# Attention, mixing FFN and top-2 attention on one core: plain float32 value products for six odd heads, an earlier start and an earlier last u

## The chip, the cores and the metric

The kernel runs on one core of a Trainium2 chip. The metric is the device time of one execution in microseconds (us), the median of the runs given. The engines are named as in the profile: PE is TensorE (matrix products; PEld its weight loads), DVE is VectorE, ACT is ScalarE, POOL is GpSimd, SP is SyncE, whose queue issues nearly all DMAs.

## The reference

Three blocks run one after another over 4 batches of 576 positions. The first is a causal attention with decay and 8 heads of 64, the second a mixing step and a feed-forward network over 512 channels, the third a top-2 gated attention of 4 experts.

```python
log_f = np.log(np.clip(f, 0.0001, 1.0)); cum = np.cumsum(log_f, axis=-1)
scores = scale * q @ k.T + cum[:, :, :, None] - cum[:, :, None, :]   # causal
attn = exp(scores - max); attn = attn / (attn.sum + 1e-09)
x = attn @ v                                                     # block 1
u = x + (x.T @ U @ V).T; x = u + np.maximum(u @ w_ch1, 0) @ w_ch2  # block 2
...                                                              # block 3: out += mask * w * ((a @ v) @ wo[e])
```

The change touches block 1 and the step from it into block 2.

## The kernel before, in words

Block 1 has 32 heads, taken in 16 pairs (`p`), an even and an odd head (`h = 2p + j`). All its work is written as events: `put(h, us, do)` (line 978) places a step at `us` in the nominal slot of 8.4 us of head `h`, `early(us, do)` (line 981) before slot 0, and the events are issued in the order of these times (line 1321). Every engine, and SP's queue, then works in that order; a time in the list decides only who stands behind whom. Slots as measured have other lengths. The pools are small: PE's results of scores and of row maxima share two buffers (`ps2`), the value product has one (`av`), the loaded q, k, v of a pair have two places.

For each head, in its slot: `score_products` (line 264) makes the transposed scores in two parts, u = 0 of 576 columns and u = 1 of two times 512; ACT takes the exponentials (line 305). Each of the three pieces is then split into float16 halves: ACT copies the high one (`high_part`, line 310), DVE subtracts it (`low_part`, line 313). In the next slot `weighted_values` (line 332) multiplies them with v, which is scaled by a power of two and split in the same way: 15 blocks, each as high by high, high by low and low by high, so 45 products of 64 or 65 columns; column 65 of v is ones and gives the sum of the row. `row_scales` and `normalise` (lines 386 and 406) divide.

v's power of two is `value_events` (line 1055): DVE's largest value (`value_max`, line 349), a transpose, three small steps on DVE (`value_power`), a product that spreads it (`value_spread`, line 369), a reciprocal, then ACT's high half and DVE's low half of both heads at once (lines 380 and 383). For pair 0 this chain, up to the spreading product, stands before slot 0.

The row maxima of head `h + 2` are made in slot `h` (`max_events`, line 1018): products `ua` and `ub` on PE (lines 202 and 220), five masked maxima on DVE (lines 207 and 228). In slot `h + 1` PE turns them (`mt`, line 234) and a DMA puts them as a row into the head's operand (`put_row`, line 237), which the scores of slot `h + 2` read. `split_events` (line 1085) prepares q and k of a pair: ACT's rounded copies, SP's moves of them between partitions (`split_moves`, line 855) and POOL's remainders.

In slots 0 to 9 PE also has `busy` products (line 1277) on a constant tile, whose results nobody reads: 8, 14 and 8 a slot. From pair 5 on, groups of block 2's first quarter (`fill`, 12 products each, lines 680 and 696) stand among the heads. After the last head comes a dense stretch of such groups. Block 2 reads u, the mixed output (`mix_events`, line 1138), which is stored to DRAM per pair and read back per batch: `ffn_begin` (line 624) reads three quarters of a batch's first half early and takes the fourth from the tile when its pair is mixed, for batches 1 and 2; batch 3 is read whole by `ffn_prepare` at the start of the dense stretch (line 1391), and `cast_some` (line 666) converts it in two pieces on ACT and DVE.

Of the kernel before, what the change touches and what calls it, by code (L numbers as in the profile page):

```python
# [18 lines left out]
P = 128  # L19
# [6 lines left out]
NT = 5  # L26
# [56 lines left out]
def kernel(  # L83
# [171 lines left out]
    def exponent_tiles(pl_, n, eng=nc.gpsimd):  # L255

        made = []
        for i in range(n):
            two = pl_.tile([P, 2 * 1600 + 64], F16, name=f"ph{i}")
            eng.memset(two[:, 3200:3264], 0.0)  # L260
            made.append((two, two[:, 1600:3264]))
        return made
# [69 lines left out]
    def weighted_values(ph, pl, vh, vl, its=(0, NT), av=None):  # L332
# [26 lines left out]
    def value_power(at_):  # L359
        counter[1] += 1  # L360
        full = ars[counter[1] % 2]
        ar = full[0:1, :]
        nc.vector.tensor_reduce(ar, at_[:], AX.X, OP.max)
        nc.vector.tensor_scalar(ar, ar, 1.0e-30, None, OP.max)
        nc.vector.tensor_scalar(ar.bitcast(I32), ar.bitcast(I32), 0x7F800000, None,
                                OP.bitwise_and)
        return full

    def value_spread(full):
        rp = psf.tile([P, 1], F32, name="rsp", tag="f")  # L370
        nc.tensor.matmul(rp[:], spread[:], full[:].bitcast(BF16)[:, 1:2], start=True, stop=True)
        return rp
# [13 lines left out]
    def row_scales(av, rs):  # L386

        den = small.tile([P, NT], F32, name="den")
        total = av()[:, :, 64:65].rearrange("p t o -> p (t o)")
        nc.vector.tensor_scalar(den[:], total, 1.0e-9 * PSCALE, rs()[:, 0:1], OP.add, OP.mult)  # L390
# [430 lines left out]
    khigh = att.tile([P, S], F32R, name="khigh")  # L821
    vhs = []
    for i in range(2):
        vh_ = hpool.tile([P, 2, NT, 65], F16, name=f"vh{i}")
        vl_ = hpool.tile([P, 2, NT, 64], F16, name=f"vl{i}")
        nc.vector.memset(vh_[:, :, :, 64:65], 1.0)
        vhs.append((vh_, vl_))
    NPAIR = B * NP
# [26 lines left out]
    def split_moves(p, j):  # L855

        if p >= NPAIR:
            return
        qa, qb, ka, kb = pair_heads(p)[j]
        src = f32(chl[2 * p + j:2 * p + j + 1]) if p < 2 else cdram[2 * p + j]  # L860
        nc.sync.dma_start(f32(ka[64:66, 0:S]), src)
        if p == j == 0:
            load_qk(1)
        if j == 0:
            nc.sync.dma_start(f32(qb[lo_, :]), f32(qa[lo_, :]))
            nc.sync.dma_start(f32(kb[hi_, :S]), f32(ka[lo_, :S]))
        else:
            nc.sync.dma_start(f32(qa[lo_, :]), f32(qb[hi_, :]))
            nc.sync.dma_start(f32(ka[lo_, :S]), f32(khigh[hi_, :]))
            nc.sync.dma_start(f32(kb[lo_, :S]), f32(khigh[hi_, :]))  # L870

# [112 lines left out]
    def head_events(h):  # L984

        p, j = divmod(h, 2)
        hb = pair_heads(p)[j]
        ph, pl = exps[h % 2]
        st = {}
# [16 lines left out]

        def attend():
            vh, vl = vhs[p % 2]
            st["av"] = weighted_values(ph, pl, vh[:, j], vl[:, j])

        put(h + 1, 4.55, attend)
        finish = row_scales(lambda: st["av"], lambda: st_rs[p])
        for us in (6.15, 6.35):
# [4 lines left out]
    def max_events(h):  # L1018
# [13 lines left out]
        if h < 2:  # L1032
            for us, n in ((8.5, 0), (8.7, 1)) if h == 0 else ((12.3, 0), (13.2, 1)):
                early(us, rows, n)
            early((9.2, 12.9)[h], lambda: last_max(st[0], st["mx"]))
            for n, t in enumerate((3, 2, 1, 0)):
                early((9.8, 13.7)[h] + 0.6 * n, first, t)
        else:
# [16 lines left out]
    def value_events(p):  # L1055
# [21 lines left out]
        put(h, 1.95, step, "am", None, value_max)  # L1077
        put(h, 4.54, step, "amt", "am", value_turn)
# [6 lines left out]
    def split_events(p):  # L1085
# [755 lines left out]
    def attend_slot(h, t, its=None, room=None, after=()):  # L1841
# [200 lines left out]
```

## Time and profile before

| what | us |
|---|---|
| median of 3 runs (lowest, highest) | 815.67 (814.83, 819.93) |
| the profiled execution, its own time | 815.98 |
| its span, first to last instruction | 814.2 |
| block 1 with its start, to the first score product / to the end of slot 12 | 17.02 / 129.57 |
| the whole first block, to the dense stretch, about | 298 |

The span is of one execution; times in the rows are from its start. A busy share counts any instruction in progress. PE's instructions overlap, so its busy time runs past the end of the streaming; the time from one start to the next is what a product costs in a stream. The releaser behind an idle time is inferred from semaphores and names what came last by the profile.

### The profile page before, as it was taken

Reading aid. Unit: us, or ns where it says so; the run is one execution under the profiler, and the core shown is the slowest. Engines: PE = TensorE matmul, PEld = TensorE weight load, DVE = VectorE, ACT = ScalarE, POOL = GpSimd, SP = SyncE. Lnnn points to the kernel's source line nnn. Section 1 sums busy time; section 2 is a strip of 40 time slices with the busy share of each in tenths; the row PEclk is TensorE's granted clock in tenths of the full one; section 3 lists DMA queues with packets and bytes.
Section 4 is the critical chain, followed back from the end, with each engine's and each line's share of the span. In section 5 each row is a group of like instructions: output and inputs, shape, how many; then the busy total and the mean of one; then the engine's idle time right before and its main releaser. Section 6 shows DMA issues by size and latency. Waiting matters only on the chain.

```text
span 814.2 us, 19790 instructions
## 1 busy us (share of the span) xinstructions
PE 763.0 (94%) x7726; PEld 658.8 (81%) x7726; DVE 605.5 (74%) x1671; ACT 433.2 (53%) x875; POOL 149.7 (18%) x248
## 2 busy tenths in 40 slices
PE   3888889999999989999899999999999889999997
PEld 3788879999999989977677777777778778888874
DVE  6988999998999948988873586366644557887873
ACT  6877887887787724637231242113311335676563
POOL 9643332423322000000002000000000511111110
PEclk9999999999999999999999999999999989999999
DMA  6565564666655044963230404400103547455422
GB/s 186 149 189 175 158 195 145 184 191 171 175 160 161 25 160 136 311 191 107 85 115 33 146 32 149 157 2 1 59 30 89 135 104 185 107 131 129 104 71 94
DMA packets 63694, 104.37 MB, mean 128 GB/s; under 512 B 5824, under 2 KB 39984, under 8 KB 63600
## 3 DMA queue, kind: packets, MB, share of 16 engines
q1 hardware_dynamic: 63232, 102.45, 42.7%
q8 instruction: 61, 1.00, 0.5%
q10 hardware_dynamic: 368, 0.66, 0.3%
q14 instruction: 33, 0.27, 0.1%
HBM read 53.25 MB, written 23.74 MB: 95 GB/s over the span
## 4 chain that ended last, share of the span: by engine, by line
PE 48%; DVE 5%; DMA 3%; ACT 1%; issue 1%; SPq 0%; ACTq 0%; DVEq 0%
PE cps L696 15%; PE hps L680 14%; PE pq L1550 5%; PE pv L1592 3%; PE sc L285 3%; PE po L1644 2%; DMA yl<-yhalves 1%; PE ub L220 1%; PE av L341 1%; PE av L345 1%; PE av L343 1%; DVE yc L702 1%; DVE w16a L537 1%; DMA ust<-udram 1%; PE ua L202 1%
## 5 line engine op out<-in xcount | busy, mean ns | idle before, releaser
L685 ACT ACTIVATE hh<-hps 128x288 f16<-128x288 f32 (+1 forms) x128 | 52.5, 410 | 221.0 <-PE hps L680 195.1
L686 DVE SCALAR_TENSOR_TENSOR hl<-hps,hh 128x288 f16<-128x288 f32 (+1 forms) x128 | 58.1, 454 | 81.6 <-ACT hh L685 81.2
L228 DVE CUSTOM_DVE_ANT_0 ub<-ub,maskm 128x448 f32<-128x448 f32 x192 | 82.2, 428 | 2.6 <-PE ub L220 1.1
L285 PE MATMUL sc<-qa,ka 128*128 128x288 f32 (+4 forms) x288 | 73.6, 316 | 4.2 <-DVE mx L207 2.2
L341 PE MATMUL av<-vh,ph 128*128 128x65 f16 x720 | 71.0, 195 | 0.3 <-DVE o L407 0.3
L343 PE MATMUL av<-vl,ph 128*128 128x64 f16 x720 | 70.6, 193 | 0.0
L345 PE MATMUL av<-vh,ph 128*128 128x65 f16 x720 | 70.5, 193 | 0.0
L702 DVE SCALAR_TENSOR_TENSOR yc<-cps,back,yc 128x288 f32<-128x288 f32 x96 | 49.4, 514 | 25.3 <-PE cps L696 22.4
L341 PEld LDWEIGHTS <-ph 128*128 128x128 f16 x720 | 65.8, 97 | 1.2 <-DVE o L407 0.6
L343 PEld LDWEIGHTS <-ph 128*128 128x128 f16 x720 | 66.1, 99 | 0.3
L345 PEld LDWEIGHTS <-ph 128*128 128x128 f16 x720 | 66.1, 98 | 0.0
L285 PE MATMUL sc<-qb,kb 128*128 128x288 f32 (+4 forms) x288 | 64.9, 307 | 0.0
L207 DVE CUSTOM_DVE_ANT_0 ua<-ua,maskm 128x576 f32<-128x576 f32 x48 | 36.5, 761 | 32.5 <-PE ua L202 27.8
L305 ACT ACTIVATE aside<-sc 128x512 f32<-128x512 f32 (+1 forms) x75 | 45.3, 617 | 26.6 <-PE sc L285 24.4
L285 PEld LDWEIGHTS sc<-qa,ka 128*128 128x128 f32 x288 | 50.0, 194 | 7.9 <-issue 3.3
L313 DVE TENSOR_TENSOR ph<-aside,ph 128x512 f16<-128x512 f32 (+1 forms) x75 | 55.1, 747 | 1.7 <-ACT ph L310 1.7
L285 PEld LDWEIGHTS sc<-qb,kb 128*128 128x128 f32 x288 | 53.6, 193 | 1.6
L313 DVE TENSOR_TENSOR ph<-pf,ph 128x512 f16<-128x512 f32 (+1 forms) x69 | 49.0, 722 | 6.4 <-ACT ph L310 6.4
L696 PE MATMUL cps<-hh,w16b 128*128 128x288 f16 x256 | 48.3, 286 | 0.8 <-DVE hl L686 0.8
L696 PE MATMUL cps<-hh,w16a 128*128 128x288 f16 x256 | 48.3, 286 | 0.0
L696 PE MATMUL cps<-hh,w1lf 128*128 128x288 f16 x256 | 48.3, 286 | 0.0
L680 PEld LDWEIGHTS <-w16a 128*128 128x128 f16 x384 | 37.4, 98 | 13.2 <-issue 3.8
(268 smaller groups left out, 2325.9 us busy)
## 6 DMA issues: line engine op xcount, KB each, us to landing
raw<-in_w_dram SPq DMA_DIRECT2D x32, 512.0 KB
ust<-udram SPq DMA_DIRECT2D x14, 576.0 KB
ydram<-yc SPq DMA_DIRECT2D x10, 576.0 KB
aside<-in_qk_dram SPq DMA_DIRECT2D x8, 576.0 KB
room<-in_qk_dram SPq DMA_DIRECT2D x8, 576.0 KB
udram<-ustage SPq DMA_DIRECT2D x16, 288.0 KB
ydram<-ust SPq DMA_DIRECT2D x8, 576.0 KB
yc<-ydram SPq DMA_DIRECT2D x8, 576.0 KB
```

Of the source, the lines that this page charges most:

```text
L228: nc.vector.tensor_tensor_reduce(ub[:, bk, off:off + w], ub[:, bk, off:off + w], maskm[:, S - w:S], 1.0, NEG, OP.add, OP.max, mx[:, t:t + 1])
L285: nc.tensor.matmul(ps[:, bk, off:off + w], wa, xa, start=bk not in banks[:n], stop=bk not in banks[n + 1:])
L305: nc.scalar.activation(pf[:, 0:S].rearrange("p (c n) -> p c n", c=2) if whole else pf[:, 0:n], view, AF.Exp, scale=ISC)
L313: nc.vector.tensor_tensor(pl[:, o0:o0 + n], pf[:, 0:n], ph[:, o0:o0 + n], OP.subtract)
L341: nc.tensor.matmul(av[:, it, :], ph[:, c:c + P], vh[:, jt, :], start=first, stop=False)
L343: nc.tensor.matmul(av[:, it, 0:64], ph[:, c:c + P], vl[:, jt, :], start=False, stop=False)
L345: nc.tensor.matmul(av[:, it, :], pl[:, c:c + P], vh[:, jt, :], start=False, stop=last)
L680: nc.tensor.matmul(ph[:], wa[:, k, fs], xa[:, k], start=n == 0, stop=n == 3 * KT - 1)
L685: after(lambda: nc.scalar.activation(hh[:], ph[:], AF.Relu), lambda: nc.vector.scalar_tensor_tensor(hl[:], ph[:], 0.0, high, OP.max, OP.su ...
L686: lambda: nc.vector.scalar_tensor_tensor(hl[:], ph[:], 0.0, high, OP.max, OP.subtract))
L696: nc.tensor.matmul(pc[:], wa[:, t, dsl], xa[:], start=n == 0, stop=n == 3 * FT - 1)
L702: nc.vector.scalar_tensor_tensor(yc[:, d, :], pc[:], back, yc[:, d, :], OP.mult, OP.add)
```

## The change

For the odd heads of pairs 0 to 5 (`NPLAIN = 6`) the exponentials are written in float32 into the tile that else holds the halves, with no split, and v's second head is loaded straight into a float32 tile with its column of ones; `plain_values` makes 15 plain float32 products, in two parts (rows 0 to 2 at 2.0 and 3 to 4 at 4.55 of the next slot). v's scale then covers the first head alone. Pair 0's scale moves from before slot 0 into slot 0, and its factor into the power step. Head 1's moves and pair 1's preparation are reordered. `busy` goes to 4 a slot, and 10 more in odd slots. `ffn_begin` also runs for batch 3.

```diff
-        nc.vector.tensor_scalar(ar, ar, 1.0e-30, None, OP.max)
+        nc.vector.tensor_scalar(ar, ar, 1.0e-30, 1.0 / VEXP, OP.max, OP.mult)
...
+    def plain_values(whole, vw, its, av=None):
+        if av is None:
+            av = ps1.tile([P, NT, 65], F32, name="av")
+        for it in range(*its):
+            order = list(range(it + 1)) if it < NT - 1 else [0, 4, 1, 2, 3]
+            for jt in order:
+                c = J_OFF[jt] + (it - jt) * P
+                nc.tensor.matmul(av[:, it, :], whole[:, c:c + P], vw[:, jt, :],
+                                 start=jt == order[0], stop=jt == order[-1])
+        return av
...
     def load_v(p):
-        if p < NPAIR:
+        if p < NPLAIN:
+            nc.sync.dma_start(places[p % 2][1][:, 0], v[p // NP, p % NP][:, 0])
+        elif p < NPAIR:
             nc.sync.dma_start(places[p % 2][1], v[p // NP, p % NP])
+    def load_second(p):
+        nc.sync.dma_start(vws[p % 2][:, 1, :, 0:64], v[p // NP, p % NP][:, 1])
...
-                st["pf", n] = exponentials(view, n_), o0, n_
+            if plain:
+                to = whole[:, o0:o0 + n_]
+                nc.scalar.activation(to if u else to.rearrange("p (c n) -> p c n", c=2), view,
+                                     AF.Exp, scale=ISC)
+            else:
+                st["pf", n] = exponentials(view, n_), o0, n_
...
             put(h, te, exp_, n)
+            if plain:
+                continue
...
-        put(h + 1, 4.55, attend)
+        if plain:
+            put(h + 1, 2.0, attend, (0, 3))
+            put(h + 1, 4.55, attend, (3, NT))
+        else:
+            put(h + 1, 4.55, attend)
...
-            early(12.6, lambda: put_row(hb, st["mt"]))
+            early(12.6, lambda: put_row(hb, st["mt"], True))
...
-            early(11.7, step, "amt", "am", value_turn)
-            early(13.9, step, "full", "amt", value_power)
-            early(14.9, step, "rp", "full", value_spread)
-            put(0, 0.2, factor)
-            put(0, 4.95, lambda: value_high(vr, st_rs[p], vh))
+            put(0, 4.54, step, "amt", "am", value_turn)
+            put(0, 5.6, step, "full", "amt", value_power)
+            put(0, 6.0, step, "rp", "full", value_spread)
+            put(0, 6.5, factor)
+            put(0, 6.6, lambda: value_high(vr, st_rs[p], vh))
...
+        if p < NPLAIN:
+            put(2 * p - 1, 4.6, load_second, p)
-    FIRST_SPLITS = ((5.8, 6.5, 7.5), (7.1, 8.8, 10.3), (11.6, 14.7, 14.8), (13.2, 19.3, 19.2))
+    FIRST_SPLITS = ((5.8, 6.5, 7.5), (7.1, 7.8, 10.3), (13.0, 14.7, 14.8), (14.2, 19.3, 19.2))
...
     for h in range(10):
-        put(h, 0.54, busy, 8)
-        put(h, 2.1, busy, 14)
-        put(h, 3.9, busy, 8)
+        put(h, 0.54, busy, 4)
+        if h % 2:
+            put(h, 2.1, busy, 10)
...
-    for b in (1, 2):
+    for b in (1, 2, 3):
         put(8 * b + 8, 4.0, ffn_begin, b)
```

On SP's queue before slot 0, the DMAs from the load of pair 0's q and k on stand in this order before (`chl` are the decay rows, `khigh` the rounded k of an odd head, `mr` the row of maxima):

```order
L836 DMA aside<-in_qk_dram 128x1152
L840 DMA aside<-in_v_dram 128x640
L861 DMA ka_130<-chl 2x1x576
L836 DMA room<-in_qk_dram 128x1152
L865 DMA qb_129<-qa_128 64x576
L866 DMA kb_131<-ka_130 64x576
L861 DMA ka_134<-chl 2x1x576
L868 DMA qa_132<-qb_133 64x576
L869 DMA ka_134<-khigh 64x576
L870 DMA kb_135<-khigh 64x576
L244 DMA qa_128<-mr 1x5x128
```

and so in the change:

```order
L856 DMA aside<-in_qk_dram 128x1152
L860 DMA aside<-in_v_dram 128x320
L892 DMA ka_128<-chl 2x1x576
L903 DMA qa_130<-qb_131 64x576
L904 DMA ka_132<-khigh 64x576
L892 DMA ka_132<-chl 2x1x576
L856 DMA room<-in_qk_dram 128x1152
L886 DMA qb_127<-qa_126 64x576
L887 DMA kb_129<-ka_128 64x576
L909 DMA kb_133<-khigh 64x576
L243 DMA qa_126<-mr 1x5x128
```

Head 1's two moves and its decay rows now stand before pair 1's load (`room`) and before head 0's two moves.

On DVE, in slot 6, from the division of head 4's output to the maxima of head 8, before (`ph_148` is the odd head's tile, `vl_161` v's low half, `am` its largest value):

```order
L407 TENSOR_TENSOR room<-av,rn 128x5x64
L938 TENSOR_TENSOR ul<-ustage,uh 128x288 x2
L313 TENSOR_TENSOR ph_148<-aside,ph_148 128x512 x2
L383 SCALAR_TENSOR_TENSOR vl_161<-aside,rs,vh_160 128x640
L351 TENSOR_REDUCE am<-room 128x1
L434 SCALAR_TENSOR_TENSOR wst<-raw,wst 128x512
L435 SCALAR_TENSOR_TENSOR wst<-raw,wst 128x512
L1242 TENSOR_TENSOR w1l<-wst,w1h 128x4x128
L313 TENSOR_TENSOR ph_146<-aside,ph_146 128x576
L207 ISA ua,mx_98<-ua,maskm 128x2x288
```

and in the change:

```order
L422 TENSOR_TENSOR room<-av,rn 128x5x64
L977 TENSOR_TENSOR ul<-ustage,uh 128x288 x2
L395 SCALAR_TENSOR_TENSOR vw_158<-aside,rs,vw_158 128x320
L363 TENSOR_REDUCE am<-room 128x1
L449 SCALAR_TENSOR_TENSOR wst<-raw,wst 128x512
L450 SCALAR_TENSOR_TENSOR wst<-raw,wst 128x512
L1304 TENSOR_TENSOR w1l<-wst,w1h 128x4x128
L313 TENSOR_TENSOR ph_144<-aside,ph_144 128x576
L206 ISA ua,mx_96<-ua,maskm 128x2x288
```

The odd head's two subtractions of 512 are gone (its third stood in the slot before), and v's low half is 320 wide.

On SP's queue at the end of the heads and the start of the dense stretch, before (`ustage` is a pair's mixed output):

```order
L943 DMA udram<-ustage 128x576 x2
L647 DMA ust<-udram 128x4x288
L546 DMA ust<-udram 128x4x288 x4
L761 DMA ydram<-ust 512x1x288
L647 DMA ust<-udram 128x4x288
L761 DMA ydram<-ust 512x1x288
```

and in the change:

```order
L982 DMA udram<-ustage 128x576
L644 DMA ust<-udram 128x3x288
L561 DMA ust<-udram 128x4x288 x4
L982 DMA udram<-ustage 128x576
L985 DMA ust<-udram 128x288
L776 DMA ydram<-ust 512x1x288
```

Three quarters of batch 3's u are read before the last pair's store, and the four loads for the other batches (line 546, 561) now stand before that store too.

## Rows read from the trace of the kernel before

**Rows 1.** The page: busy time of each engine in the span.

```profile
PE 763.0 (94%) x7726; PEld 658.8 (81%) x7726; DVE 605.5 (74%) x1671; ACT 433.2 (53%) x875; POOL 149.7 (18%) x248
```

**Rows 2.** Busy time by stretch, slots 0 to 12; columns: us, engines, PEclk, DMA share, GB/s.

```profile
17.02:23.91 6.89, 6.89 (x56) 6.55 (x55) 4.02 (x11) 3.57 (x7) 5.91 (x8) 1.00 0.71 203
23.91:33.28 9.37, 6.67 (x104) 6.06 (x101) 8.94 (x23) 8.47 (x18) 6.71 (x8) 1.00 0.61 175
33.28:50.30 17.02, 14.86 (x217) 13.87 (x218) 14.91 (x47) 12.53 (x26) 8.11 (x8) 1.00 0.51 140
50.30:65.77 15.47, 14.38 (x220) 13.72 (x219) 14.30 (x44) 13.26 (x28) 5.61 (x5) 1.00 0.68 197
65.77:84.78 19.01, 16.39 (x220) 15.33 (x218) 16.78 (x48) 15.13 (x31) 6.10 (x5) 0.91 0.55 160
84.78:102.24 17.46, 14.84 (x220) 13.82 (x218) 16.70 (x48) 15.17 (x32) 6.12 (x5) 1.00 0.61 175
102.24:121.95 19.71, 16.19 (x195) 15.12 (x194) 19.00 (x57) 17.40 (x37) 7.04 (x5) 1.00 0.65 195
121.95:129.57 7.62, 7.62 (x95) 7.49 (x95) 7.52 (x17) 6.26 (x13) 2.02 (x2) 1.00 0.48 135
```

**Rows 3.** Waits of PE, 23 to 123 us: us in total, times, longest.

```profile
PE mt L234 <- DVE mx L228: 7.6, 7, 1.5
```

**Rows 4.** PE's products: timeline (start, us, [idle]) and groups by form (busy, mean ns).

```profile
60.34 0.94 PE L1280 MATMUL some<-every 128*128 128x128 bf16 x14
61.13 1.28 PE L895 MATMUL gp<-room,ut 128*96 128x128 f32 x10
63.53 0.21 PE L341 MATMUL av<-vh,ph 128*128 128x65 f16 x1
64.91 0.41 PE L912 MATMUL up<-ident,room 128*128 128x128 f32 x2
...
L895 PE MATMUL gp<-room,ut 128*96 128x128 f32 x80 | 10.1, 273 | 0.0
L285 PEld LDWEIGHTS sc<-qb,kb 128*128 128x128 f32 x288 | 53.6, 193 | 1.6
```

**Rows 5.** DVE in slot 6 (timeline), and ACT's high copies in slots 1 to 11 (group).

```profile
68.28 0.68 DVE L313 TENSOR_TENSOR ph<-aside,ph 128x512 f16<-128x512 f32 x1
68.88 0.88 DVE L383 SCALAR_TENSOR_TENSOR vl<-room,rs,vh 128x640 f16<-128x640 f32 x1
69.68 0.81 DVE L351 TENSOR_REDUCE am<-aside 128x1 f32<-128x640 f32 x1
...
L310 ACT CAST ph<-aside 128x512 f16<-128x512 f32 x16 | 9.7, 619 | 0.0
```

**Rows 6.** The start: timelines of PE, SP's queue and ACT.

```profile
13.93 0.82 PE L202 MATMUL ua<-ka,qa 127*128 127x288 f32 x2 [1.23 <-POOL ka L167]
16.92 0.16 PE L371 MATMUL rsp<-ar,spread 128*128 128x1 bf16 x1 [1.26 <-DVE ar L365]
...
7.28 0.35 SPq L836 DMA_DIRECT2D room<-in_qk_dram  x1
10.23 0.55 SPq L869 DMA_DIRECT2D ka<-khigh  x1
...
21.93 0.60 ACT L305 ACTIVATE aside<-sc 128x512 f32<-128x512 f32 x1 [1.41 <-PE sc L285]
```

**Rows 7.** PE's first score product of slot 12.

```profile
121.95 0.37 PE L285 MATMUL sc<-qa,ka 128*128 128x288 f32 x1 [1.30 <-DMA qa<-mr]
```

**Rows 8.** The start of the dense stretch: SP's queue, ACT, PE, and a stretch as in rows 2.

```profile
297.39 0.60 SPq L647 DMA_DIRECT2D ust<-udram  x1
...
301.91 1.24 ACT L670 CAST uh<-ust 128x576 fp32r<-128x576 f32 x2 [3.43 <-DMA ust<-udram]
...
303.97 0.16 PE L482 MATMUL rsp<-ar,every 128*128 128x1 bf16 x1 [2.63 <-DVE ar L477]
...
305.06:308.47 3.41, 3.41 (x16) 3.41 (x16) 2.06 (x8) 0.00 (x0) 0.00 (x0) 0.50 0.79 280
```

More of the change, by code (lines that the diff above doesn't have):

```diff
@@ L44 @@
 FIRST = 15.6
+NPLAIN = 6
 PER_PAIR = (0,) * 5 + (3, 3, 3, 3, 4, 4, 4, 4, 3, 3, 2)
@@ L128 @@
     nc.gpsimd.memset(every[:], 1.0)
-    spread = const.tile([P, P], BF16, name="spread")
-    nc.gpsimd.memset(spread[:], 1.0 / VEXP)
     ars = []
@@ L258, in exponent_tiles @@
         for i in range(n):
-            two = pl_.tile([P, 2 * 1600 + 64], F16, name=f"ph{i}")
-            eng.memset(two[:, 3200:3264], 0.0)
-            made.append((two, two[:, 1600:3264]))
+            one_ = pl_.tile([P, 1664], F32, name=f"ph{i}")
+            eng.memset(one_[:, 1600:1664], 0.0)
+            two = one_[:].bitcast(F16)
+            made.append((two, two[:, 1600:3264], one_))
         return made
@@ L370, in value_spread @@
         rp = psf.tile([P, 1], F32, name="rsp", tag="f")
-        nc.tensor.matmul(rp[:], spread[:], full[:].bitcast(BF16)[:, 1:2], start=True, stop=True)
+        nc.tensor.matmul(rp[:], every[:], full[:].bitcast(BF16)[:, 1:2], start=True, stop=True)
         return rp
@@ L389, in row_scales @@
         total = av()[:, :, 64:65].rearrange("p t o -> p (t o)")
-        nc.vector.tensor_scalar(den[:], total, 1.0e-9 * PSCALE, rs()[:, 0:1], OP.add, OP.mult)
+        if rs() is None:
+            nc.vector.tensor_scalar(den[:], total, 1.0e-9 * PSCALE, None, OP.add)
+        else:
+            nc.vector.tensor_scalar(den[:], total, 1.0e-9 * PSCALE, rs()[:, 0:1], OP.add, OP.mult)
         yield
@@ L821 @@
     khigh = att.tile([P, S], F32R, name="khigh")
-    vhs = []
+    vhs, vws, firsts = [], [], []
     for i in range(2):
[L824 to L827, printed above, removed]
+        v_ = hpool.tile([P, 2 * NT * 65], F32, name=f"vw{i}")
+        vws.append(v_[:].rearrange("p (a t d) -> p a t d", a=2, t=NT))
+        nc.vector.memset(vws[i][:, 1, :, 64:65], 1.0)
+        n0, n1 = 2 * NT * 65, 2 * NT * (65 + 64)
+        vhs.append((v_[:].bitcast(F16)[:, 0:n0].rearrange("p (a t d) -> p a t d", a=2, t=NT),
+                    v_[:].bitcast(F16)[:, n0:n1].rearrange("p (a t d) -> p a t d", a=2, t=NT)))
+        firsts.append([v_[:].bitcast(F16)[:, n * NT:(n + k) * NT].rearrange(
+            "p (a t d) -> p a t d", a=1, t=NT) for n, k in ((0, 65), (65, 64))])
+        nc.vector.memset(firsts[i][0][:, :, :, 64:65], 1.0)
     NPAIR = B * NP
@@ L858, in split_moves, with rows @@
             return
+        if j == 2:
+            qa, qb, ka, kb = pair_heads(p)[0]
+            nc.sync.dma_start(f32(qb[lo_, :]), f32(qa[lo_, :]))
+            nc.sync.dma_start(f32(kb[hi_, :S]), f32(ka[lo_, :S]))
+            return
         qa, qb, ka, kb = pair_heads(p)[j]
         src = f32(chl[2 * p + j:2 * p + j + 1]) if p < 2 else cdram[2 * p + j]
-        nc.sync.dma_start(f32(ka[64:66, 0:S]), src)
-        if p == j == 0:
-            load_qk(1)
+        def rows():
+            nc.sync.dma_start(f32(ka[64:66, 0:S]), src)
         if j == 0:
+            rows()
+            if p == 0:
+                return
             nc.sync.dma_start(f32(qb[lo_, :]), f32(qa[lo_, :]))
             nc.sync.dma_start(f32(kb[hi_, :S]), f32(ka[lo_, :S]))
[L867 to L870, printed above, removed]
+            return
+        if p:
+            rows()
+        nc.sync.dma_start(f32(qa[lo_, :]), f32(qb[hi_, :]))
+        nc.sync.dma_start(f32(ka[lo_, :S]), f32(khigh[hi_, :]))
+        if p == 0:
+            rows()
+            load_qk(1)
+            split_moves(0, 2)
+        nc.sync.dma_start(f32(kb[lo_, :S]), f32(khigh[hi_, :]))
     def split_low(p, j, which=(0, 1)):
@@ L987, in head_events @@
         hb = pair_heads(p)[j]
-        ph, pl = exps[h % 2]
+        ph, pl, whole = exps[h % 2]
+        plain = j == 1 and p < NPLAIN
         st = {}
@@ L1032, in max_events @@
         if h < 2:
-            for us, n in ((8.5, 0), (8.7, 1)) if h == 0 else ((12.3, 0), (13.2, 1)):
+            for us, n in ((8.5, 0), (8.7, 1)) if h == 0 else ((11.3, 0), (12.3, 1)):
                 early(us, rows, n)
-            early((9.2, 12.9)[h], lambda: last_max(st[0], st["mx"]))
+            early((9.2, 12.45)[h], lambda: last_max(st[0], st["mx"]))
             for n, t in enumerate((3, 2, 1, 0)):
-                early((9.8, 13.7)[h] + 0.6 * n, first, t)
+                early((9.8, 13.1)[h] + 0.6 * n, first, t)
         else:
```

28 lines of the change are left out of this document (19 added, 9 removed).

## The prediction, made before the changed kernel was run

> **What bounds the kernel now.** I read each engine's share of the span first (PE 94%) [rows 1], then its busy time in stretches cut where TensorE (PE) begins a head's scores, which I call slots [rows 2], then what PE waited for in them [rows 3]. From slot 12 on PE is the bound: 7.62 us busy of 7.62. In slots 1 to 11 no engine is full alone: in slots 8 and 9 VectorE (DVE) is busy 16.70 of 17.46 us, ScalarE (ACT) 15.17, PE 14.84. PE's longest wait there is for the row maxima that DVE writes: 7.6 us in 7 waits, 1.5 at most [rows 3]. So these slots are set by DVE, with PE standing behind it, and part of PE's busy time is filling: 300 `busy` products in slots 0 to 9, at 0.056 us 16.8 in all [rows 4]. Two more places count. Before slot 0, PE waits for a move of head 1 and then for a chain on v's scale [rows 6]. At the end of the attention PE stands still for 2.63 us and then runs at the lower clock level [rows 8].
>
> **What the change costs and saves, part by part.** All sums are against the profiled execution, 815.98 us (span 814.2); the median of the runs shown is 815.67, 0.3 less, inside their spread of 5 us.
>
> *Engine loads of a pair of slots.* On PE the six odd heads give up 45 float16 products for 15 float32 ones. The 45 take 1.38 us, from the first start to that of the transposes behind them (63.53 to 64.91) [rows 4]. The nearest float32 row is the mixing product with U: its five products stand in the trace as ten passes, each with its own weight load. Ten passes take 1.28 us, and with the last one's own 0.27 taken off that is 0.112 a step, the first of them being longer than the rest; I read 0.11. Those passes stream 128 columns and load 96 of weights; the new ones stream 65 and load 128. If a pass went by its columns it would take 0.055; if load and stream did not overlap, the load's 0.193 [rows 4]. I take 0.11, the nearest row: 30 x 0.11 = 3.3, so 1.9 us more per odd head.
>
> The row shows float32 loads of 0.193 us against float16 products that start 0.031 us apart. [...]
>
> The `busy` products go from 30 a slot to 4 in even and 14 in odd slots: 42 fewer per pair, 0.056 each by 0.94 us for 14 of them with a tail of 0.16 [rows 4], 2.35 us less. Net on PE per pair: -0.45.
>
> On DVE each odd head loses its three subtractions: 512 wide they start 0.60 apart (68.28 to 68.88), the 576 wide one an eighth more, 1.87 together; v's low part (0.80 from start to start) and its largest value (0.81, of which such rows overlap 0.08) are made on half the columns [rows 5], 0.76 less. That is 2.6 us less per pair. ACT loses three copies of 0.62 or a little more [rows 5]: about 1.9.
>
> So per pair, in us, PE / DVE after the change: slots 2+3 14.4 / 12.3, slots 4+5 13.9 / 11.7, slots 6+7 14.2 / 14.2 (PE there also loses the 1.7 that the lower clock cost: granted 0.91 over 19 us), slots 8+9 14.4 / 14.1 [rows 2]. Now the largest load takes 96% of the pair in slots 8+9 and as little as 88% in slots 2+3 and 6+7. With 88% the four pairs take 64.6 us, with 100% 56.9, against 68.96 now: a gain of 4.3 to 12.1. I take 96%, since the waits of PE for the maxima come in the slots where DVE still has the odd head's subtractions before them, and just these go: 59.5 us, **9.4 gained**.
>
> *Start and slot 0.* PE's rows of head 1 begin at 13.93. The row names a fill on GpSimd, but that is another head's tile; what they read last is the move of khigh, which SP issued at 10.23. Then PE waits until 16.92 for the product that spreads v's scale, behind head 1's maxima on DVE, and the first scores follow at 17.02 [rows 6]. The change issues head 1's moves ahead of the next pair's 576 KB load (7.28 now) and of head 0's own moves, and takes v's scale into slot 0. Head 1's rows can begin some 2 us sooner; the first scores then wait for head 0's moves, two or three issues later than now, and for the row of maxima, issued as late as now. I put them near 15.4. The first exponential comes hardly sooner, because the next pair's load, and with it ACT's four conversions ahead of that exponential, goes out about 3 us later. The second one, at 21.93, waits for scores that PE begins behind 8 `busy` products, of which 4 go, at the lower clock; it should come near 19.7. So slot 1 begins **2.0 sooner** (0 to 3). Two v loads more stand on SP's queue ahead of pair 1's moves: about 1 us, inside that range. Later each second v load stands on that queue between a weight block and the next heads' moves; it waits for a product of the slot before, and v has a slot or more in hand, so I cost it at nothing; were that cover gone, it would be its own issue, half a microsecond a pair.
>
> *Slot 1.* DVE 8.94 of 9.37 us; a subtraction of 576 and half of v's low part go, about 1.07: **1.1 gained** (0 to 1.1).
>
> *Slots 10 and 11.* No `busy` products here, so PE gets 16.19 + 1.9 = 18.1 of the 19.71; the first scores of slot 12 wait 1.30 us for a move of head 12's maxima [rows 7] behind two 576 KB loads of u. **1.0 gained** (0 to 1.6).
>
> *Slot 12.* PE is busy throughout, and takes head 11's float32 product: **1.9 lost** (0 to 1.9). Slots 13 to 31 do not change.
>
> *The last batch's u.* Now SP issues its load at 297.39, ACT's conversion waits for it until 301.91, DVE's subtraction behind that, and a factor that PE needs stands behind this on DVE; PE starts again at 303.97 after 2.63 us and runs 3.41 us at 0.50 [rows 8], which is 1.7 us of work. With the change the first three quarters are read while the last heads run, and the fourth is converted from the tile itself, so that no conversion waits: **4.3 gained** (0 to 4.3). What is late next on SP is the last pair's store and the read of its own quarter, which now stand behind four loads of 576 KB; what they feed is only added at the end of that batch's step, some 30 us later.
>
> Sum: 2.0 + 1.1 + 9.4 + 1.0 - 1.9 + 4.3 = 15.9, so 815.98 - 15.9 = **800.1 us**.
>
> **Rivals.**
>
> *The engines keep waiting for one another* (88% of the pair): the pairs gain 4.3 and slot 1 nothing: 815.98 - 9.7 = 806.3. For it: no engine is full in slots 2 to 9 now [rows 2], and with PE and DVE nearly equal afterwards each has less slack to catch up after a wait. Against: slot 12 and the slots like it run with PE full beside a DVE at 7.52 of 7.62 [rows 2].
>
> *The float32 pass is paced by an exposed load*, 0.193: 2.5 us more per odd head than I took. In four pairs at 96% 10.5, in slots 10 and 11 the 1.0 gained and 0.9 more, in slot 12 2.5: 14.9 in all, 815.0, no change. For it: the load's own time. Against: in the mixing rows a load of much the same kind repeats every 0.11 [rows 4], so loads overlap there.
>
> [...]
>
> *The last part does nothing*: u is there, but the stall moves to the next factor or the next load, which stand on the same queue: 800.1 + 4.3 = 804.4.
>
> **How the numbers follow.** The forecast's case gets 0.60, the engines' waits 0.17, the last part 0.10, the exposed load 0.07, the clock 0.06. The likeliest is 800.1. The best ends of the terms give 3 + 1.1 + 12.1 + 1.6 - 1.9 + 4.3 = 20.2, 795.8, and a pass at 0.055 some 3 more, so the low end is 793; the high end is 810, which takes in the waits and the last part, and leaves out the exposed load and the clock, 0.13. One per cent (8.2 us, about what a measurement of this kernel can tell from no change) lies at 807.5: faster holds the forecast, the last part and most of the waits, 0.85; the same the rest of the waits and most of the exposed load, 0.09; slower the clock, 0.06.
>
> **What would show it.** Right: slots 2 to 9 near 59.5 us in all, with PE's waits for the maxima nearly gone; products of an odd head starting about 0.11 apart in 30 passes; the first scores near 15.4; slot 12 about 1.9 longer; no wait of PE above 1 us near the end of the attention and no 0.50 behind it. Wrong: a granted clock under 0.9 in slots 1 to 9; passes near 0.055 or 0.19; DVE below 85% and PE below 90% busy in slots 6 to 9 alike, with waits between them; or a new wait for u's loads after the attention.

## The result, and the profile after

Four runs of the changed kernel took 800.21 to 804.82 us, median 804.0, beside a median of 816.3 for the kernel before: ratio 0.985 (95% interval 0.9817 to 0.9882). Six further runs (below) gave 800.9 to 809.34, median 802.55, ratio 0.9832 (0.9797 to 0.9866). The forecast was 800.1, with 793 to 810 as its range. The profiled execution took 804.72, its span is 803.0.

The page's first part of the changed kernel, which answers to [rows 1]:

```profile
PE 763.5 (95%) x7426; PEld 659.8 (82%) x7426; DVE 589.6 (73%) x1656; ACT 422.6 (53%) x858; POOL 148.7 (19%) x247
```

Its busy time by stretch, slots 0 to 13, columns as in [rows 2]:

```profile
15.82:23.61 7.79, 5.78 (x31) 5.04 (x32) 3.33 (x10) 7.18 (x14) 7.05 (x9) 0.99 0.88 256
23.61:31.39 7.78, 7.11 (x85) 6.34 (x85) 6.91 (x23) 5.82 (x12) 6.78 (x8) 0.79 0.69 197
31.39:51.58 20.19, 18.91 (x161) 17.96 (x161) 11.21 (x42) 10.00 (x21) 7.92 (x8) 0.75 0.42 115
51.58:65.32 13.74, 13.70 (x162) 13.25 (x161) 12.10 (x41) 11.63 (x25) 5.54 (x5) 1.00 0.67 194
65.32:80.40 15.08, 14.10 (x162) 13.29 (x161) 14.65 (x46) 13.30 (x28) 5.79 (x5) 1.00 0.76 208
80.40:95.50 15.10, 14.12 (x162) 13.30 (x161) 14.62 (x46) 13.31 (x28) 5.66 (x5) 1.00 0.75 210
95.50:113.25 17.75, 17.63 (x180) 17.05 (x179) 15.49 (x49) 14.80 (x31) 5.86 (x5) 1.00 0.84 229
113.25:122.94 9.69, 9.62 (x81) 9.35 (x80) 8.96 (x31) 7.08 (x15) 3.40 (x3) 1.00 0.49 129
122.94:131.03 8.09, 8.08 (x102) 7.71 (x100) 5.64 (x16) 6.39 (x13) 1.65 (x2) 1.00 0.44 144
```

The third row is the odd one. Slots 4+5, 6+7 and 8+9 came down to 13.74, 15.08 and 15.10 us, but slots 2+3 went up to 20.19 from 17.02 [rows 2], at a mean granted clock of 0.75: it was 0.50 for 10.2 us from 37.1 on. What PE waited for from 23 to 115 us, which answers to [rows 3]:

```profile
PE ub L219 <- ACT aside L305: 2.1, 2, 1.2
PE rsp L383 <- DVE ar L377: 1.1, 1, 1.1
PE ub L219 <- ACT pf L305: 0.9, 1, 0.9
PE sc L285 <- DMA qa<-mr: 0.4, 1, 0.4
PE ub L219 <- ACT ph L1039: 0.3, 1, 0.3
```

The 7.6 us of waits for DVE's row maxima are gone. A new one stands in the second line: the product that spreads v's scale waits for DVE's factor. The sum by stretch, each stretch from PE's first score product of one head to that of another (the last column is a second profiled execution of the same kernel, span 800.3, from the run e9_change_again below):

| us | before | forecast | after | after, second execution |
|---|---|---|---|---|
| until slot 1 begins | 23.91 | 21.9 | 23.61 | 23.57 |
| slot 1 | 9.37 | 8.3 | 7.78 | 7.82 |
| slots 2 to 9 | 68.96 | 59.5 | 64.11 | 59.39 |
| slots 10+11 | 19.71 | 18.7 | 17.75 | 17.74 |
| slot 12 | 7.61 | 9.5 | 9.69 | 9.70 |
| slot 13 | 8.88 | 8.9 | 8.08 | 8.08 |
| slots 14 to 30 | 140.4 | 140.4 | 140.6 | 140.6 |
| from slot 31 to the end | 535.3 | 531.0 | 531.4 | 533.5 |

The dense stretch begins without its stall. PE's row there, the wait for it from 272 to 330 us (total, times, longest), and SP's queue, which answer to [rows 8]:

```profile
293.91 0.18 PE L497 MATMUL rsp<-ar,every 128*128 128x1 bf16 x1
...
PE rsp L497 <- DVE ar L492: 0.6, 1, 0.6
```

```profile
281.41 0.38 SPq L644 DMA_DIRECT2D ust<-udram  x1
281.96 2.66 SPq L561 DMA_DIRECT2D ust<-udram  x4
288.07 0.33 SPq L982 DMA_DIRECT2D udram<-ustage  x1
```

The 2.63 us before that product are down to 0.6, no 0.50 follows, and the last pair's store does stand behind the four loads, as forecast, with no wait of PE for what it feeds.

### The profile page after: what moved, and what is told of

Its sections match the earlier page's. It is cut to its first block, busy times and chain, and to the rows that moved or that the text cites. A ratio compares the mean times of both kernels' runs of the same rounds, so it can differ in the third digit from the quotient of the medians.

```text
span 803.0 us, 19172 instructions
## 1 busy us (share of the span) xinstructions
PE 763.5 (95%) x7426; PEld 659.8 (82%) x7426; DVE 589.6 (73%) x1656; ACT 422.6 (53%) x858; POOL 148.7 (19%) x247
## 4 chain that ended last, share of the span: by engine, by line
PE 49%; DVE 5%; DMA 2%; ACT 1%; issue 0%; SPq 0%; ACTq 0%; DVEq 0%
PE cps L711 15%; PE hps L695 15%; PE pq L1612 6%; PE pv L1654 3%; PE sc L285 3%; PE po L1706 2%; PE ub L219 1%; PE av L341 1%; PE av L345 1%; PE av L343 1%; DMA ust<-udram 1%; DVE yc L717 1%; DMA qa<-hq 1%; DVE w16a L552 1%; PE ua L201 1%; DMA kb<-hk 1%
## 5 line engine op out<-in xcount | busy, mean ns | idle before, releaser
L341 PEld LDWEIGHTS <-ph 128*128 128x128 f16 x630 | 57.5, 97 | 1.2 <-DVE o L422 0.6
L343 PEld LDWEIGHTS <-ph 128*128 128x128 f16 x630 | 57.9, 98 | 0.2
L345 PEld LDWEIGHTS <-ph 128*128 128x128 f16 x630 | 57.9, 97 | 0.0
L313 DVE TENSOR_TENSOR ph<-pf,ph 128x512 f16<-128x512 f32 (+1 forms) x65 | 46.2, 723 | 6.4 <-ACT ph L310 6.4
L695 PEld LDWEIGHTS <-w16a 128*128 128x128 f16 x384 | 37.4, 98 | 14.4 <-issue 5.0
L313 DVE TENSOR_TENSOR ph<-aside,ph 128x512 f16<-128x512 f32 (+1 forms) x61 | 45.0, 749 | 3.1 <-ACT ph L310 3.1
L1840 POOL TENSOR_SCALAR_AFFINE_SELECT pf<-pf 128x128 f32<-128x128 f32 (+1 forms) x80 | 23.7, 317 | 122.7 <-ACT pf L305 122.1
L711 PEld LDWEIGHTS <-w16b 128*128 128x128 f16 x384 | 37.6, 98 | 10.6 <-issue 1.1
L305 ACT ACTIVATE aside<-sc 128x512 f32<-128x512 f32 (+1 forms) x61 | 36.7, 617 | 17.5 <-PE sc L285 15.6
L695 PEld LDWEIGHTS <-w1hf 128*128 128x128 f16 x384 | 37.5, 98 | 9.4
```

Source lines behind the costliest of these rows:

```text
L313: nc.vector.tensor_tensor(pl[:, o0:o0 + n], pf[:, 0:n], ph[:, o0:o0 + n], OP.subtract)
L341: nc.tensor.matmul(av[:, it, :], ph[:, c:c + P], vh[:, jt, :], start=first, stop=False)
L343: nc.tensor.matmul(av[:, it, 0:64], ph[:, c:c + P], vl[:, jt, :], start=False, stop=False)
L345: nc.tensor.matmul(av[:, it, :], pl[:, c:c + P], vh[:, jt, :], start=False, stop=last)
L695: nc.tensor.matmul(ph[:], wa[:, k, fs], xa[:, k], start=n == 0, stop=n == 3 * KT - 1)
L711: nc.tensor.matmul(pc[:], wa[:, t, dsl], xa[:], start=n == 0, stop=n == 3 * FT - 1)
```

## The experiments

All runs are compared with the kernel before on the same chip. Its median was 815.76 us for the first four kernels, 814.63 for the next four and 816.15 for the last four.

**The old number of fillers.**

```diff
-        put(h, 0.54, busy, 4)
-        if h % 2:
-            put(h, 2.1, busy, 10)
+        put(h, 0.54, busy, 8)
+        put(h, 2.1, busy, 14)
+        put(h, 3.9, busy, 8)
```

> The changed kernel with the old number of fillers, 30 in each of slots 0 to 9. In the changed kernel's profile (804.72 us) the granted clock is 0.50 from 23.3 to 26.8 and from 37.1 to 47.2 us. Theory A, the missing fillers let the clock fall: it stays at 1.00 in slots 0 to 9, slots 2+3 go from 20.19 to about 15 us, and what the fillers cost in slots 4 to 9, where PE is 93 to 100% busy, takes 3 to 6 us back: 800 to 803 us. Theory B, the clock falls because PE waits for ACT's exponentials in slot 2 and for v's scale in slot 0, whatever the fillers do: 0.50 is seen at the same places, slots 4 to 9 get longer all the same, 808 to 811 us.

Measured: 807.88 us, ratio 0.9899 (0.9858 to 0.9939). Slots 2 to 9 and slots 4 to 9:

```profile
31.49:95.81 64.32, 64.32 (x808) 62.44 (x809) 53.75 (x170) 48.65 (x99) 25.00 (x19) 1.00 0.63 183
47.74:95.81 48.07, 48.07 (x608) 46.75 (x607) 41.24 (x129) 38.66 (x79) 16.92 (x13) 1.00 0.66 193
```

No fall of the clock, as theory A had it, but the time misses its 800 to 803: PE is busy for every one of the 64.32 us, so with the plain products and all the fillers it is the bound. Slots 4 to 9 take 48.07 against 43.92 in the changed kernel (PE busy for 41.92), 4.15 more, and most of what the clock gave back is spent there.

**The old fillers in slots 0 to 3 only** (the same three lines under `if h < 4:`, then `continue`).

> The changed kernel with the old 30 fillers in slots 0 to 3 only; slots 4 to 9 keep the new, smaller number. Theory A (missing fillers let the clock fall): clock 1.00 from slot 0 to slot 9, slots 2+3 near 15 us, slots 4 to 9 as in the changed kernel (43.9 us), 798 to 800 us. Theory B (the waits alone do it): 0.50 stays in slots 1 to 3, 804 to 807 us.

Measured: 805.61 us, 0.9869 (0.9834 to 0.9905). Slots 2 to 9 took 61.60 us with one stretch of 3.4 us at 0.50 in slot 2, in spite of 30 fillers in it. Neither theory as put: the falls are shorter (3.4 us at 0.50 instead of 10.2 in slots 2 and 3) but not gone, and the time lies in theory B's range, so nothing was won that can be measured.

**The kernel before with the new, smaller number of fillers** (the first diff the other way round, in the kernel before).

> The kernel before with the new, smaller number of fillers and nothing else changed. Theory A (fillers hold the clock): stretches at 0.50 appear in slots 0 to 9, 10 us or more in all, and since PE is not full there half of their cost is hidden by DVE: 818 to 823 us. Theory B (fillers only take PE time): no new stretch at 0.50, and the time goes down by up to 4 us, 812 to 816.

Measured: 819.37 us (815.6 to 826.8, ten runs), 1.0048 (1.002 to 1.0077). The mean granted clock of its ten runs is 0.977 to 0.986, that of 19 runs of the kernel before on the same chip 0.988 to 0.997. Three slots of its profile, and its slots 4 to 9:

```profile
23.27:33.15 9.88, 8.20 (x88) 7.76 (x87) 9.23 (x24) 8.96 (x18) 6.99 (x8) 0.65 0.57 175
64.10:73.26 9.16, 6.62 (x77) 5.89 (x75) 8.40 (x21) 9.07 (x20) 3.55 (x3) 0.81 0.52 152
81.60:90.40 8.80, 6.52 (x77) 5.90 (x75) 8.45 (x22) 8.70 (x19) 3.25 (x2) 0.81 0.55 157
...
49.12:98.74 49.62, 40.31 (x528) 37.10 (x526) 47.65 (x138) 43.62 (x88) 18.36 (x14) 0.93 0.62 185
```

Theory A holds in the old kernel: with DVE as the bound and PE waiting, fewer fillers came with new stretches at 0.50 in slots 1, 6 and 8. What they cost shows in the median alone, 3.6 us above the kernel before: the profiled execution is the fastest of the ten (815.60 us), and its slots 4 to 9 are 2.3 us shorter than before in spite of 6.8 us at 0.50.

**The last batch's u alone, in the kernel before.**

```diff
-    for b in (1, 2):
+    for b in (1, 2, 3):
         put(8 * b + 8, 4.0, ffn_begin, b)
```

> The kernel before, with the last batch's u begun early and nothing else changed. Forecast: the wait of 2.63 us after the attention and the 3.41 us at 0.50 behind it go, 3.9 to 4.3 us less, 811.5 to 812.5 us by the median of before near 816. Rival (the part does nothing by itself, the stall moves to the next load): within 1 us of before.

Measured: 812.91 us, 0.9955 (0.9926 to 0.9984). From the first score product of slot 31 to one product in the dense stretch, 52.46 us before and 48.18 now, 4.28 less. There the forecast holds, and this part works by itself. The median fell by 2.85 us, so it misses the forecast 811.5 to 812.5 by 0.4, well inside the spread of the single times.

**v's scale of pair 0 back ahead of slot 0.**

```diff
-            put(0, 4.54, step, "amt", "am", value_turn)
-            put(0, 5.6, step, "full", "amt", value_power)
-            put(0, 6.0, step, "rp", "full", value_spread)
-            put(0, 6.5, factor)
-            put(0, 6.6, lambda: value_high(vr, st_rs[p], vh))
+            early(11.7, step, "amt", "am", value_turn)
+            early(13.9, step, "full", "amt", value_power)
+            early(14.9, step, "rp", "full", value_spread)
+            put(0, 0.2, factor)
+            put(0, 4.95, lambda: value_high(vr, st_rs[p], vh))
```

> The changed kernel with pair 0's v scale put back ahead of slot 0, where it stands in the kernel before; all else as changed. Theory (the start's term was mis-sized because this chain, moved into slot 0, makes PE wait 1.1 us for DVE's factor at the end of slot 0): that wait goes, the first scores stay near 15.8 us, slot 1 begins at 22.2 to 22.7 instead of 23.61, and the time falls by about 1 us. Rival (slot 0's length is set by ACT and the DMAs of head 2's rows, not by this chain): the wait moves to the row of maxima that slot 2 needs from DMA, slot 2 begins within 0.5 us of 31.39, and the time is unchanged within 1 us.

Measured: 800.57 us (800.35 to 801.14), 0.9827 (0.98 to 0.9854). Slot 1 begins at 23.00, slot 2 at 30.62 instead of 31.39. The theory had slot 1 at 22.2 to 22.7, the rival slot 2 within 0.5 us of 31.39; neither came. The rows that explain it are, in the changed kernel, DVE, SP's queue, PE and ACT's second exponential:

```profile
25.91 0.96 DVE L395 SCALAR_TENSOR_TENSOR vw<-aside,rs,vw 128x320 f16<-128x320 f32 x1 [0.63 <-ACT vw L392]
```

```profile
26.91 0.37 SPq L860 DMA_DIRECT2D aside<-in_v_dram  x1
27.37 0.37 SPq L856 DMA_DIRECT2D room<-in_qk_dram  x1
27.84 0.79 SPq L243 DMA_DIRECT2D qa<-mr  x1
```

```profile
23.51 0.16 PE L383 MATMUL rsp<-ar,every 128*128 128x1 bf16 x1 [1.14 <-DVE ar L377]
31.39 0.37 PE L285 MATMUL sc<-qa,ka 128*128 128x288 f32 x1 [0.38 <-DMA qa<-mr]
...
20.26 0.60 ACT L305 ACTIVATE aside<-sc 128x512 f32<-128x512 f32 x1 [0.53 <-PE sc L285]
```

and with the scale put back, DVE, SP's queue and PE:

```profile
24.78 0.77 DVE L395 SCALAR_TENSOR_TENSOR vw<-aside,rs,vw 128x320 f16<-128x320 f32 x1 [0.23 <-ACT vw L392]
...
25.57 0.37 SPq L860 DMA_DIRECT2D aside<-in_v_dram  x1
26.04 0.39 SPq L856 DMA_DIRECT2D room<-in_qk_dram  x1
26.52 0.78 SPq L243 DMA_DIRECT2D qa<-mr  x1
...
23.00 0.58 PE L285 MATMUL sc<-qa,ka 128*128 128x288 f32 x1 [0.89 <-DVE ar L375]
```

Besides making PE wait, the late scale delays the conversion of pair 0's v, which frees the place that pair 2's v is loaded into. That load stands on SP's queue ahead of head 2's row of maxima, and the scores of slot 2 wait for that row. With the scale put back the row goes out 1.32 us sooner, and in these two executions slot 1 begins 0.61 and slot 2 0.77 us sooner; the first product of slot 1 still waits 0.89 us for DVE. The wait for the factor (0.9 to 1.1 us) and the late row (out at 27.7 to 28.4 us) are in all seven profiled executions with the late scale. What they cost is not shown by one pair of executions: the run with the halved products (below), which up to slot 2 is the changed kernel with the late scale, begins slot 1 at 23.05 and slot 2 at 30.66.

**Five plain heads instead of six** (`NPLAIN = 5`).

> The changed kernel with five plain odd heads instead of six: head 11 goes back to float16 halves. Theory (slot 12 has PE full and pays the longer product there): slot 12 falls from 9.69 to about 7.7 us, slots 10+11 go from 17.75 to 18.5 or 19.5 since DVE and ACT take the subtractions and copies of head 11 again, slot 13 goes back to 8.9; the sum of slots 10 to 13 within 1 us of 35.5, and the time within 1 us of the changed kernel. Rival (the sixth head is pure loss): slots 10 to 13 shorter by 1.5 us or more.

Measured: 800.72 us, 0.983 (0.9804 to 0.9856), so no difference from six. Slots 10+11 took 17.74, slots 12+13 17.64, together 35.38 against 35.53 with six. Slots 10+11 did not grow to the 18.5 or 19.5 expected, and slot 12 fell to 8.24, not to 7.7. The sixth plain head pays in slot 12 what it saves in slot 13.

**Each plain product as two, of half the columns.**

```diff
-                nc.tensor.matmul(av[:, it, :], whole[:, c:c + P], vw[:, jt, :],
-                                 start=jt == order[0], stop=jt == order[-1])
+        for c0, c1 in ((0, 33), (33, 65)):
+            ...
+                nc.tensor.matmul(av[:, it, c0:c1], whole[:, c:c + P], vw[:, jt, c0:c1],
+                                 start=jt == order[0], stop=jt == order[-1])
```

> The changed kernel with each plain float32 product made as two, of columns 0 to 32 and 33 to 64, so 60 passes per head instead of 30, each streaming half of the columns and loading the same 128 by 128 weights. In the changed kernel a pass takes 0.112 us at full clock. Theory A (the weight load paces a pass): a pass stays near 0.11, an odd head's product doubles to 6.6 us, the odd and even slots 4 to 9 grow by about 3 us a pair, 10 us or more in all with slots 2, 10 and 12: 818 to 825 us. Theory B (load and streaming one after the other, 128 and twice 65 columns): a pass falls to about 0.08, a head's product is 4.9 us, 809 to 815 us. Theory C (columns alone): 0.056 and no change in time.

Measured: 829.06 and 838.32 us. An odd head's product in the changed kernel, slot 6, each part with the row behind it:

```profile
67.54 1.50 PE L357 MATMUL av<-vw,ph 128*128 128x65 f32 x12
68.85 0.51 PE L201 MATMUL ua<-ka,qa 127*128 127x288 f32 x2
...
71.02 2.12 PE L357 MATMUL av<-vw,ph 128*128 128x65 f32 x18
72.94 0.38 PE L285 MATMUL sc<-qa,ka 128*128 128x288 f32 x1
```

12 passes in 1.31 us and 18 in 1.92, so 0.109 and 0.107 a pass. With half the columns, in slot 6 and in slot 4:

```profile
80.60 2.82 PE L358 MATMUL av<-vw,ph 128*128 128x33 f32 x24
83.26 0.51 PE L201 MATMUL ua<-ka,qa 127*128 127x288 f32 x2
```

```profile
61.21 7.73 PE L358 MATMUL av<-vw,ph 128*128 128x33 f32 x36
68.75 0.59 PE L285 MATMUL sc<-qa,ka 128*128 128x288 f32 x1
```

24 passes in 2.66 us are 0.111 each: half the columns change nothing, so theories B and C are out. That the weight load paces the pass (theory A) fits, but is not shown: every pass here loads 128 by 128 weights, so a cost that each pass pays alike would fit too, and no run tells the two apart. The time rose further than theory A said because the clock fell as well: slot 4's 36 passes took 7.54 us, 0.209 each, and its row reads

```profile
55.05:68.75 13.70, 13.70 (x92) 13.59 (x90) 5.71 (x20) 6.93 (x15) 3.83 (x3) 0.70 0.53 160
```

with PE busy for all of its 13.70 us; the granted clock was 0.50 from 60.5 us to its end.

**Fillers where PE waits** (12 more in even slots 0 to 8, at 3.9, between the two groups of row-maximum products).

> The changed kernel with 12 fillers more in even slots 0 to 8, between the two groups of row-maximum products, where PE waits 0.9 to 1.4 us for ACT. Theory A (the clock falls where PE waits and fillers are few): 0.50 is not seen in slots 2 and 3, or for 3.4 us at most, slots 2+3 take 15 to 17 us instead of 20.19, slots 4 to 9 stay within 0.5 us of 43.9; 798 to 802 us. Theory B (the fall has to do with something else than PE's waits): the granted clock is as in the changed kernel, 803 to 806 us.

Measured: 802.18 us, 0.9847 (0.9822 to 0.9873), with slots 2+3 in 15.87 us, slots 2 to 9 in 60.67 and no 0.50 there. Clock and slots 2+3 are as theory A had them; slots 4 to 9 took 44.80 us, more than its 43.9 and 0.5, and the time is just above its 802. But the change itself had no fall there in its second execution (below), without these fillers, and its ratio was the same (0.9832), so this run decides nothing.

**The change itself, once more.**

> The changed kernel itself, run again. Theory A (its loss against the forecast is a fall of the granted clock in slots 2 and 3 that comes in some executions and not in others): slots 2+3 take 15 to 16.5 us in an execution without the fall and about 20 with it, the single times spread over 4 to 5 us, with a median of 801 to 804. Theory B (the fall belongs to this order of work): 10 us at 0.50 in slots 2 and 3 again, slots 2+3 near 20.2, times within 1.5 us of 804.

Measured: 802.55 us, 800.9 to 809.34. Slots 2+3, and slots 2 to 9:

```profile
31.39:46.85 15.46, 14.26 (x166) 13.35 (x163) 12.69 (x42) 10.02 (x22) 8.72 (x8) 1.00 0.57 155
...
31.39:90.78 59.39, 56.19 (x646) 53.21 (x643) 54.07 (x170) 48.25 (x100) 25.71 (x20) 1.00 0.68 192
```

Theory A: the same program, with slot 2 begun at the same 31.39, took 20.19 us for slots 2+3 in one execution and 15.46 in another. The spread of its times, 8.4 us, is wider than theory A said. Over all ten executions of the changed kernel time and clock go together: the five from 800.21 to 803.05 us have a mean granted clock of 0.994 to 0.996, the five from 803.28 to 809.34 one of 0.986 to 0.991.

**The new order of the start alone, in the kernel before** (head 1's moves and maxima as in the change; scale, products and fillers as before).

> The kernel before with the new order of the start alone: head 1's moves ahead of pair 1's load, its maxima sooner; v's scale stays ahead of slot 0, the products are in float16 halves, the fillers as before. Theory (the start's own gain is real, 1.5 to 2 us, and reaches the end as long as nothing in slot 1 takes it back): slot 2 begins at 31.2 to 31.9 instead of 33.28 and the time falls by 1.5 to 2 us against the kernel before. Rival (DVE, which is busy 8.9 of 9.4 us in slot 1, sets slot 2's start whatever stands before): slot 2 within 0.5 us of 33.28, the time unchanged within 1 us.

Measured: 815.21 us, 0.9978 (0.9952 to 1.0003), no difference that can be told. Slot 1 begins at 23.11 and slot 2 at 32.26, 0.8 and 1.0 sooner than before: less than the theory, more than the rival. Slot 1 took 9.15 us and 9.37 before, so it took nothing back; what is missing was lost ahead of it.

**v's scale still sooner** (turn at 9.3, power at 11.8, spread at 12.4; otherwise as with the scale put back).

> The changed kernel with pair 0's v scale ahead of slot 0 and sooner than in the kernel before: the transpose behind head 0's row-maximum products, the spreading product behind head 1's. Forecast: PE waits for no factor of pair 0, neither before slot 0 nor in it; first scores at 15.4 to 15.8 us, but ACT is still behind pair 1's four conversions and its table load until 18 us, so slot 1 begins no more than 0.5 us ahead of the 23.00 of the version with the scale put back; 800 to 801 us. Rival (the first scores set the start): slot 1 at 22.2 or sooner, 799 to 800.

Measured: 802.09 us, 0.9808 (0.9779 to 0.9838). The first scores came at 15.23 and slot 1 at 22.57, but slot 2 at 31.63: in this execution PE's products took their longer form (0.45 us for one of 288 columns, 0.29 later) until 30.4, nearly to the end of slot 1, which lasted 9.06 us with PE busy for 8.74. Neither expectation can be read from it.

**No fillers at all, with the scale put back.**

> The changed kernel with v's scale put back ahead of slot 0 and no fillers at all. Theory A (fillers hold the clock, and the 90 that are left are needed): stretches at 0.50 of 10 us or more in slots 0 to 9, slots 2 to 9 take 62 to 66 us instead of 58.8, 804 to 808 us, with a wide spread. Theory B (the useful work holds it by itself): no more than 3.4 us at 0.50, and slots 2 to 9 shorter by the 2 to 3 us that the remaining fillers take where PE is full: 797 to 799 us.

Measured: 799.44 us (798.72 to 799.55, four runs), 0.9779 (0.975 to 0.9807), the lowest of all and, by both edits together, 3.1 us below the change on the same chip. Slots 0+1 and slots 2 to 9:

```profile
16.82:33.61 16.79, 14.57 (x96) 12.84 (x96) 10.76 (x29) 13.79 (x27) 14.96 (x18) 1.00 0.75 215
33.61:91.13 57.52, 53.52 (x573) 50.52 (x570) 52.89 (x168) 47.45 (x97) 24.46 (x19) 1.00 0.67 193
```

Theory B for slots 2 to 9: 57.52 us and no fall, 1.3 less than with 90 fillers (58.79), where 2 to 3 were expected. Slots 0+1 took 2.3 us more than the 14.48 of the version with the scale put back, for the clock, read from the length of PE's products (last section), rose only at 35.9 us, in slot 2.

## Why the prediction was right, and where it was not

The mechanism held, and the sum nearly: 800.1 forecast, 804.0 and 802.55 measured, so that 12.3 and 13.6 us came of the 15.9, by the medians. That it is so near is in part luck: in the second execution the start and the last u gave 4.1 us less than forecast, slot 1 and slots 10 to 13 2.0 more. By its own steps:

- **The pairs** (9.4 forecast). Without a fall of the clock 9.6 were gained (59.39), and PE was busy 14.10 and 14.12 us in slots 6+7 and 8+9, where 14.2 and 14.4 were forecast. The profiled execution gained 4.85, and the rest went in slots 2+3, where the clock of 0.75 is a sign of being wrong that the prediction names. The chances have the clock as the case that ends slower, at 0.06, and no run of the change shows it: the slowest of the change's ten executions took 809.34 us, beside a median of 816.15 before. What came in slots 2+3 was a fall in one of the two profiled executions: 10.2 us at 0.50 cost the difference of 20.19 and 15.46, 4.7 us.
- **What in it earns the time.** Slots 4 to 9 took 51.94 us before, 49.62 with fewer fillers alone, 48.07 with plain heads alone and 43.92 with both (3.4 and 6.8 us at 0.50 are in the first two). Each alone gains 2.3 or 3.9, both together 8.0; with the start or the last u alone these slots stay at 51.91 and 51.93. The 43.92 is no chance: in six profiled executions with the plain heads and the new fillers it is 43.92 to 43.95. But in the old kernel, where PE waits for DVE, with fewer fillers the mean granted clock was 0.977 to 0.986 instead of 0.988 to 0.997 and the median 3.6 us higher; in the new one, with PE nearly full (41.92 of 43.92 us), four executions (798.72 to 799.55) show no need of even the last 90.
- **A float32 pass** (0.11 forecast): 0.107 to 0.109. The 0.055 end is out, as a pass did not go by its columns (0.111 with 33 of them), and so is the exposed load of 0.193. These are passes at a granted clock of 1.00; at 0.50, in slot 4 with the halved products, 36 passes took 0.209 each.
- **The start** (2.0 forecast, 0.3 measured until slot 1; 3.1 against 1.9 until slot 2, as slot 1 itself gained 1.6, not 1.1). The second exponential came at 20.26, near the 19.7 forecast, but slot 1 did not follow it as closely as before. The step that failed is "takes v's scale into slot 0", to which I gave a gain and no price. PE waits 1.14 us for the factor at the end of slot 0, and SP's queue holds head 2's maxima behind a load that waits for the late conversion. How much of the missing 1.7 us this is stays open: with the scale put back slot 1 began at 23.00, with another wait for DVE, but an execution with the late scale began it at 23.05; and no version began it sooner than 22.57, 1.3 ahead of the kernel before, so 2.0 was too much in any case. In the time the scale's place can't be told, 0.9827 against 0.9832.
- **Slots 10 to 13** (0.9 lost forecast, 0.67 gained). The size of slot 12's loss was right, 2.1 against 1.9. Slots 10+11 gained 2.0 instead of 1.0 (0 to 1.6): the 1.30 us wait for head 12's maxima went too, and PE is busy 17.63 us of 17.75. Slot 13, which I left unchanged, gave 0.8 back.
- **The last u** (4.3 forecast): 4.3 at a product of the dense stretch by itself in the old kernel, 3.5 and 3.9 at the same product in the two executions of the changed one, where 0.6 and 0.2 us of the wait remained.
- **The end.** In both executions of the change 1.3 to 1.4 us of that are lost again inside block 2, where the run without fillers loses none. To the end they keep 3.9 and 1.8, a difference of 2.1, and 1.7 of it (half of 3.4 us) is the clock at the end of block 2: 3.4 us at 0.50 in the first, 6.8 in the second as in the kernel before, which the change does not touch. So the 3.9, near the forecast, are in part luck.

Why the clock fell in slot 2 of one execution and not of the other stays open. The work in front of it was alike: 12 plain passes, two row-maximum products, then a wait for ACT of 1.15 us in the one and 1.03 in the other. The products behind that wait, in the first execution and in the second:

```profile
36.95 1.16 PE L219 MATMUL ub<-ka,qa 127*128 127x448 f32 x4 [1.15 <-ACT aside L305]
38.10 3.94 PE L357 MATMUL av<-vw,ph 128*128 128x65 f32 x18
...
36.82 0.76 PE L219 MATMUL ub<-ka,qa 127*128 127x448 f32 x4 [1.03 <-ACT aside L305]
37.53 2.12 PE L357 MATMUL av<-vw,ph 128*128 128x65 f32 x18
```

## What to carry to other kernels

Work that fills an engine for its clock's sake is to be priced anew when a change makes that engine the bound: here the old number of fillers then cost 4.15 us in slots 4 to 9, and the run with none was the fastest (799.44). While another engine is still the bound, taking it out can cost more than it gives, as in the kernel before (3.6 us in the median). When a short chain is moved later, follow what its result frees, and price it: here a buffer, a load into it, and on the same queue a small transfer that the next scores wait for. One profile of a kernel whose clock falls in some executions shows one draw (20.19 or 15.46 us for the same slots here); a second execution, cut into the same stretches, tells a loss that belongs to the program from one that does not.

## What was not expected of the hardware

PE ran at 0.50 while its records show it busy throughout: 13.70 of 13.70 us in slot 4 (55.05 to 68.75) with the halved products. The clock fell at 60.5 us, with no idle time of PE in the slot before it (busy 9.23 of 9.23 us, 45.82 to 55.05), so waits alone do not explain this fall.

The clock column reads 1.00 for slots 0+1 without fillers (16.82 to 33.61), yet the same product of 288 columns is seen at two lengths:

```profile
33.99 0.44 PE L285 MATMUL sc<-qb,kb 128*128 128x288 f32 x1
...
41.16 0.29 PE L285 MATMUL sc<-qb,kb 128*128 128x288 f32 x1
```

Up to 35.9 us all such products took the longer time, which in the changed kernel is their length where the column reads 0.50 (0.44 us at 24.23). So ahead of the first change of the clock that the profile records, the level is read from the length of a known product and not from the column. By that measure PE first came to full speed at 19 us in the run with 30 fillers in each of slots 0 to 3 and at 22 in the kernel before; with fewer at 20 and 28 in the change's two executions, at 19 with the scale put back and at 30.4 with the scale still sooner; and at 35.9 with none.
